# Wider token chunks in a two-FFN kernel, with a table of shifts for the order of its instructions

## The chip, the cores and the metric

The kernel runs on one core of one Trainium2 chip. The metric is the device time of one execution in microseconds (us), as a median of several runs. The engines are named as the profile names them: PE (TensorE, matmuls; PEld its weight loads), DVE (VectorE), ACT (ScalarE), POOL (GpSimd) and SP (SyncE, which here only starts DMAs). All of them run at the same time, each with a queue of instructions in a fixed order.

## The reference

Attention is followed by two feed-forward networks (FFNs) on the same 2304 tokens (4 batches of 576).

```python
scores = where(block_i >= block_j, q @ k.T / 8, -1e9)   # 4 x 8 heads, 576 tokens, 64 wide, blocks of 64
x = softmax(scores) @ v                                 # -> [2304, 512]
h = x @ w_in                                            # first FFN, 512 -> 1024
solu = h * softmax(h)
ln = (solu - mean) / sqrt(var + 1e-6) * g_ln
x = ln @ w_out                                          # 1024 -> 512
h = x @ w_in2                                           # second FFN, 512 -> 2048
out = (h * sigmoid(1.702 * h)) @ w_out2                 # 2048 -> 512
```

The inputs are handed over as 64-bit floats for the weights, so each weight matrix has to be put together from two 32-bit words on the chip. Both FFNs are computed with each operand as a sum of a high and a low part (H and L), three matmuls for one product: H by H, H by L and L by H.

## The kernel before

**How it is scheduled.** The program isn't issued as it is written. A class `Recorder` takes every operation with a priority (`_add`, L294; the priority is a time in us at which the work is due), and `issue` (L418) replays them through a model: `_cost` (L222) estimates each instruction, `HOP` the time of a semaphore between engines, `_room` (L114) gives out the 8 banks of PSUM, and of all operations the one with the earliest modelled start goes next, by priority where they tie. The result is a fixed order on each engine. Operations that can run on several engines (`copy`, `both`, `affine`) go to the one that the model sees done first. While the model is below `WARM` = 100 us, `_keep_busy` (L398) puts in idle 128-column matmuls, which read the tile `mask` and compute nothing, wherever the model sees PE without work for over 0.4 us. Because everything goes through `Recorder`, nearly every instruction stands under one line, L387, in the profile; tiles tell them apart.

**Attention** (`attention`, L986). 16 pairs of heads, four for each batch. `load_qk` (L709) and `load_v` load a pair; for the first batch first the tokens up to 256, then the rest, one pair after the other on SP's queue, and pair 0's k alone on ACT's. `scores` computes the products, `u_pt` transposes the softmax, `u_pv` multiplies with v. Raw q and k stand in four buffers (`rawb`, L602; the last one lies in the tile `x_all` of the first FFN).

**First FFN** (`first_ffn`, L1057). 18 tiles of 128 tokens. `h_mm` multiplies one tile with `w_in` (24 matmuls of 512 columns), `solu_ln` does the activation and the norm, `ln_t` (L955) transposes the tile into `lnTb`, and `y_mm` (L972) multiplies a chunk of `CH` = 256 tokens (two tiles) with `w_out`: for each of 9 chunks four calls of 24 matmuls, 256 columns each. Its result goes through the tiles `yo` to DRAM (`y1d`). Weights are converted by `w1_prep` through the landing tiles `e` and the tiles `wtmp` (L576).

**Second FFN.** Tokens go in four chunks, `sizes = [640, 512, 512, 640]` (L1135), and the 2048 hidden columns in 8 pairs of 256. A chunk of n tokens and one pair is computed by a scheme with 7 products instead of 8 (`h2_steps`, L1270): each product is 6 matmuls over half a chunk, n/2 columns, into one bank of PSUM, and DVE or ACT then reads it out (tiles `p`, `u`, `hc`); the activation goes through `sg` to the tiles `g` (H and L). `out_steps` (L1319) multiplies `g` with `w_out2`: for each 128 tokens of the chunk 6 matmuls of 512 columns, which accumulate over four pairs in one bank that is held for so long. The products of pair p+1 and the output steps of pair p are recorded interleaved. The pairs 0 to 3 go over all chunks in order first, then the pairs 4 to 7 over the chunks in reverse order. Where the chunk changes, `y_split` (L1253) writes the seven operands of the next one into their only set of tiles. `prep_w2` (L1215) makes the weights of a pair, `ahead` (L1197) converts those of later pairs and parks them in DRAM (`w2d`). There are three sets of `g` tiles (L1174, L1378), two or three `hc` and two `p`.

Of the kernel before, what the change touches and what calls it, by code (L numbers as in the profile page):

```python
# [2 lines left out]

# [18 lines left out]
def full(t):  # L22
    return t.bitcast(F32)

# [35 lines left out]
class Recorder:  # L60
# [5 lines left out]
    HOP = 0.06  # L66
    SPAN = 10
    OWN = 0.15
    LEAVE = (0, 1, 1)
    WARM = 100.0  # L70
    IDLE = 0.4
    SWITCH = 0.09
# [5 lines left out]
    def __init__(self, tc, banks):  # L78
# [4 lines left out]
        self.n_buf = 0  # L83
        self.places = {}
# [24 lines left out]
    def bank(self, level, n=1, name="b"):  # L109
        self.n_buf += 1  # L110
        b = Buf(n, level, f"{name} {self.n_buf}")
        return Bank(b, self.banks, (lambda t: t[:, 0]) if n == 1 else (lambda t: t[:, 0:n]))
# [109 lines left out]
    def _cost(self, eng, name, kw, outs, ins):  # L222


        out = kw.get("out")
        n = out.free_size() if callable(out.free_size) else out.free_size
        sb = [a for a in ins if a.space != PSUM]
        if eng == "tensor":
            if name == "transpose":
                return 0.109, 0.2, False  # L230
            k = kw["lhsT"].shape[0]
            if kw["lhsT"].dtype == F32:

                return max(0.109, 0.87 * n / 1000), 0.3 + (0.87 * n / 1000 if k == 64 else 0.0), False
            if k == 64:
                return max(0.054, 0.235 * n / 1000), 0.17 + 0.427 * n / 1000, False
            return max(0.109, 0.008 + 0.435 * n / 1000), 0.17 + 0.0 * n, False
        if name == "dma_start":
            return 0.48, 1.9, False
        if eng == "scalar":  # L240
            m = max((a.free_size() if callable(a.free_size) else a.free_size) for a in ins)
            c = 0.18 + 0.81 * m / 1000
            if kw["in_"].space != PSUM:
                c += 0.04
            if hasattr(kw.get("bias"), "partition_size"):
                c += 0.08
            if kw.get("accum_out") is not None:
                c += 0.19
            return c - 0.09, 0.09, False
        m = max([n] + [(a.free_size() if callable(a.free_size) else a.free_size) for a in ins])  # L250
        if eng == "vector":
            if name == "memset":
                return 0.06 + m / 1000, 0.05, False
            two = [a for k, a in kw.items() if k in ("in0", "in1", "in_") and a.space != PSUM
                   and (a.free_size() if callable(a.free_size) else a.free_size) > 1]
            port = len(two) == 2 or (len(two) == 1 and name in ("tensor_copy", "tensor_scalar"))
            c = 0.10 + 1.04 * m / 1000
            if kw.get("accum_out") is not None:
                c += 0.08
            return c, 0.07, port  # L260
        if name == "memset":
            return 0.07 + m / 1000, 0.05, False
        if name == "tensor_tensor":
            if kw["op"] == ALU.pow:
                return 0.55, 0.05, True
            return 0.2 + 2.4 * m / 1000, 0.05, True
        return 0.1 + 1.2 * m / 1000, 0.05, True
# [26 lines left out]
    def _add(self, forms):  # L294
# [7 lines left out]
        op.prio = self.prio  # L302
# [50 lines left out]
    def _wake(self, i):  # L353
        op = self.ops[i]
        op.ready = {}
        for e in op.forms:
            t = 0.0
            for eng, done, lag, _ in op.after:
                if eng == e:
                    t = max(t, done - lag if e == "tensor" else done)  # L360
                else:
                    t = max(t, done + self.HOP)
# [35 lines left out]
    def _keep_busy(self, mode, start):  # L398

        t = max(self.free["tensor"], 0.6)  # L400
        if self.idle is None or t > self.WARM:
# [100 lines left out]
def kernel(  # L502
# [29 lines left out]
    CH = 256  # L532
    TPC = CH // 128
    NC = NT // CH
# [12 lines left out]
    y1d = [dram.tile([DM, CH], F32, name=f"y1d{c}") for c in range(NC)]  # L547

    begun = const.tile([128, 1], F32, name="begun")
    tc.nc.scalar.activation(out=begun, in_=mhalf, func=ACTF.Exp)  # L550
# [6 lines left out]
    w1i_all = keep.tile([128, 2 * KD, FF1], F32R, name="w1i")  # L557
# [4 lines left out]
    x_all = keep.tile([128, 2560], F32, name="x")  # L562
    xs_all = keep.tile([128, 2048], F32R, name="xs")
    xb = [x_all[:, i * 512:i * 512 + 512].rearrange("p (k n) -> p k n", k=KD) for i in range(2)]
    rb = [mp.tile([128, KD, 128], F32, name=f"r{i}") for i in range(2)]
# [4 lines left out]
    eb = [mp.tile([128, 2, 512], F32, name=f"e{i}") for i in range(3)]  # L570
# [3 lines left out]
    yo_all = mp.tile([128, 3 * CH], F32, name="yo")  # L574
    yob = [yo_all[:, i * CH:(i + 1) * CH] for i in range(3)]
    wtmp = [yo_all[:, 0:512].bitcast(I32), junk.rearrange("p a b -> p (a b)").bitcast(I32)]  # L576
# [20 lines left out]

    NPTY = 1
# [3 lines left out]
    rawb = [ap1.tile([128, 2, S], F32, name=f"rawqk{i}") for i in range(3)]  # L602
    rawb.append(x_all[:, 1024:1024 + 2 * S].rearrange("p (n s) -> p n s", n=2))
# [12 lines left out]
    ptx = ap1.tile([128, 2, 384], F32, name="ptx")  # L616
# [14 lines left out]
    def ptx_of(p):  # L631

        return ptyb[0][:, :, 384 * (p - 1):384 * p] if early(p) else ptx
# [9 lines left out]
    def clear():  # L643
        nc.vector.memset(mask, 0.0)
        nc.idle = mask
        nc.vector.memset(mask[0:64, 448:512], -1e30)
        for t in vb:
# [78 lines left out]
    def split_qk(p):  # L726
# [4 lines left out]
        r = rawb[vat(p)]  # L731
# [72 lines left out]
    def scores(p, what):  # L804
# [4 lines left out]
        if p < NFULL:  # L809
            terms = [(rawb[vat(p)][:, 0], rawb[vat(p)][:, 1])]  # L810
# [144 lines left out]
    def ln_t(t, half):  # L955
# [3 lines left out]
        i = t % TPC  # L959
# [12 lines left out]
    def y_mm(cc, m):  # L972
        y = nc.bank(0, name="y")[:, 0:CH]
        H, L = lnTb
# [493 lines left out]
```

## Time and profile before

| what | us |
|---|---|
| median of 3 runs (lowest to highest) | 773.4 (772.5 to 773.99) |
| the profiled execution | 772.48 |
| its span, first to last instruction | 770.7 |
| PE busy | 763.0 |
| DVE, ACT, POOL busy | 526.6, 438.2, 288.2 |
| granted TensorE clock, share of full | 0.999 |

The profiled execution is one run; 1.8 us of it lie outside the span of the instructions. A matmul's busy time in the profile is longer than the distance to the next one, because matmuls overlap; the distance between starts is what they cost. Three stages can be told apart by the tiles: attention with the first FFN until about 260 us, the first FFN alone until about 377 us (its last `y_mm` run between the first products of the second FFN until 392 us), then the second FFN.

### The profile page before, as it was taken

The page shows a single profiled execution, that of the slowest core. Times are in us where ns is not written, and L with a number is a line of the kernel's source. Part 1 is how long each engine was busy: PE and PEld are TensorE (multiplying, and loading weights), DVE is VectorE, ACT ScalarE, POOL GpSimd, SP SyncE. Part 2 cuts the span into 40 slices and gives each one's busy share as a digit, 9 for nine tenths or more (in the row PEclk, how much of TensorE's full clock was granted, in tenths as well). Part 3 has the DMA queues.
Part 4 walks back from the last instruction along what each step waited for, and adds up shares of the span by engine and source line. Part 5 has one row for each costly group of instructions (what it writes and reads, how often), then busy time and mean ns, then how long its engine had stood idle before and what let it go on. Part 6 is the DMA issues. An engine that isn't in the chain of part 4 may idle for free.

```text
span 770.7 us, 14020 instructions
## 1 busy us (share of the span) xinstructions
PE 763.0 (99%) x4994; PEld 655.3 (85%) x4994; DVE 526.6 (68%) x1203; ACT 438.2 (57%) x1001; POOL 288.2 (37%) x359
## 2 busy tenths in 40 slices
PE   9999999999999999999999999999999999999998
PEld 6576777887878889989999899988899989999886
DVE  4989848557566578698458877668977564667544
ACT  6978957767675657567345645454555442435321
POOL 3525501223331264354122445464443221535311
PEclk9999999999999999999999999999999999999999
DMA  8876523531211346554502364456423030130201
GB/s 257 260 235 185 187 89 121 158 113 54 80 57 53 112 121 168 177 163 147 171 21 74 94 202 147 141 158 218 133 82 95 14 110 14 56 110 1 96 1 68
DMA packets 81431, 91.43 MB, mean 119 GB/s; under 512 B 11089, under 2 KB 58321, under 8 KB 81361
## 3 DMA queue, kind: packets, MB, share of 16 engines
q1 hardware_dynamic: 81216, 90.41, 38.0%
q8 instruction: 39, 0.64, 0.4%
q14 instruction: 32, 0.25, 0.1%
q10 hardware_dynamic: 144, 0.13, 0.1%
HBM read 66.59 MB, written 23.93 MB: 117 GB/s over the span
## 4 chain that ended last, share of the span: by engine, by line
PE 94%; ACT 1%; DMA 1%; DVE 1%; POOL 1%; issue 1%; SPq 0%; ACTq 0%; DVEq 0%
PE PS L387 94%; DMA land<-in_moe_w_out_dram 1%; ACT P L387 1%; DMA e<-in_moe_w_out_dram 0%; DVE w1o L387 0%; POOL xs L387 0%; POOL yo L387 0%; POOL e L387 0%; ACT e L387 0%; ACT pty L387 0%; POOL sg L387 0%; DVE e L387 0%; DVE ob L387 0%; DVE wt L387 0%; ACT wt L387 0%
## 5 line engine op out<-in xcount | busy, mean ns | idle before, releaser
L387 ACT ACTIVATE sg<-hc 128x320 f32<-128x320 f32 (+1 forms) x128 | 56.5, 442 | 108.4 <-DVE hc L387 94.3
L387 PE MATMUL PS<-w2oL,gH 128*128 128x512 f32 x288 | 113.1, 393 | 0.0
L387 PE MATMUL PS<-w2oH,gH 128*128 128x512 f32 x288 | 113.0, 392 | 0.0
L387 PE MATMUL PS<-w2oH,gL 128*128 128x512 f32 x288 | 112.1, 389 | 0.0
L387 PE MATMUL PS<-lnTH,w1o 128*128 128x256 f32 x576 | 109.3, 284 | 0.0
L387 PE MATMUL PS<-w1i,xs 128*128 128x512 f32 x432 | 108.4, 399 | 0.0
L387 PE MATMUL PS<-w1i,w2SH 128*128 128x320 f32 (+1 forms) x512 | 105.1, 295 | 0.0
L387 POOL TENSOR_TENSOR sg<-hc,sg 128x256 f32<-128x256 f32 (+1 forms) x54 | 46.1, 854 | 128.8 <-ACT sg L387 128.7
L387 PEld LDWEIGHTS PS<-w1i,xs 128*128 128x128 f32 x432 | 78.2, 188 | 17.2 <-issue 2.1
L387 PEld LDWEIGHTS PS<-lnTH,w1o 128*128 128x128 f32 x576 | 90.6, 188 | 1.6 <-issue 0.7
L387 PEld LDWEIGHTS PS<-w1i,w2SH 128*128 128x128 f32 x512 | 85.1, 190 | 3.8
L387 PE MATMUL PS<-lnTL,w1o 128*128 128x256 f32 x288 | 81.2, 282 | 0.0
L387 DVE TENSOR_TENSOR hc<-PS,u 128x320 f32<-128x320 f32 (+1 forms) x96 | 43.7, 456 | 52.9 <-PE PS L387 48.2
L387 DVE CUSTOM_DVE_ANT_0 P<-PS,mask 128x512 f32<-128x512 f32 (+3 forms) x128 | 57.1, 485 | 30.9 <-PE PS L387 30.6
L387 PE MATMUL PS<-w1i,w2SL 128*128 128x320 f32 (+1 forms) x256 | 75.8, 296 | 0.0
L387 ACT ACTIVATE P<-P,mx 128x256 f32<-128x256 f32 (+3 forms) x128 | 70.3, 551 | 9.0 <-DVE mx L387 8.9
L387 ACT ACTIVATE gH<-sg 128x320 fp32r<-128x320 f32 (+1 forms) x114 | 49.8, 442 | 32.3 <-DVE sg L387 24.8
L387 PEld LDWEIGHTS PS<-w2oH,gL 128*128 128x128 f32 x288 | 54.1, 188 | 12.5 <-DVE gL L387 0.6
L387 PEld LDWEIGHTS PS<-w2oH,gH 128*128 128x128 f32 x288 | 54.2, 188 | 9.0
L387 PEld LDWEIGHTS PS<-w2oL,gH 128*128 128x128 f32 x288 | 54.2, 188 | 8.1
L387 POOL TENSOR_TENSOR gL<-sg,gH 128x256 fp32r<-128x256 f32 (+1 forms) x44 | 36.6, 838 | 52.1 <-ACT gH L387 51.3
L387 DVE TENSOR_TENSOR gL<-sg,gH 128x320 fp32r<-128x320 f32 (+1 forms) x84 | 47.8, 574 | 11.5 <-ACT gH L387 9.8
(193 smaller groups left out, 1660.1 us busy)
## 6 DMA issues: line engine op xcount, KB each, us to landing
land<-in_moe_w_in_dram SPq DMA_DIRECT2D x16, 512.0 KB, 3.9
land<-in_moe_w_out_dram SPq DMA_DIRECT2D x16, 512.0 KB, 4.4
w2d<-wt SPq DMA_DIRECT2D x24, 256.0 KB, 2.2
wt<-w2d SPq DMA_DIRECT2D x24, 256.0 KB, 2.9
x<-y1d SPq DMA_DIRECT2D x10, 512.0 KB, 6.1
y1d<-yo SPq DMA_DIRECT2D x36, 128.0 KB, 1.9
e<-in_moe_w_in_dram SPq DMA_DIRECT2D x8, 512.0 KB, 4.2
r<-rcd SPq DMA_DIRECT2D x32, 128.0 KB, 3.8
```

The costliest lines, as they stand in the source:

```text
L387: getattr(getattr(self.nc, e), name)(*map(real, args), **{k: real(v) for k, v in kw.items()})
```

## The change

- `sizes` becomes three chunks of 768 tokens. A product then has 384 columns, and the output steps hold 6 banks of PSUM, which leaves two: `_room` gets a rule that at most two products are alive at a time, in the order in which they are recorded, in place of leaving one bank free.
- `TILES = [2, 2, 2, 3, 3, 3, 3]`: `y_mm` works on chunks of 256 or 384 tokens, 7 instead of 9. There are two `yo` tiles instead of three.
- The first loads: for the four pairs of the first batch q goes on SP's and k on ACT's queue, all q and k come ahead of all v, and the first activation (with the load of its table) is recorded behind them.
- To make room, tiles share memory: raw q and k have two tiles of their own and two in `x_all`, pairs from 4 on alternate between two; one of the `wtmp` lies in the x tile of the first FFN; `ptx` and the `r` tiles lie in `x_all`; the small tiles of the second FFN lie in the `e` tiles; there are two sets of `g` and one `p`. One output weight of pair 1 is parked in DRAM.
- The model's costs are changed (`_cost`, a `HOPS` for each engine, `SWITCH`), idle matmuls may be put in at any time (they read `ident` after the attention), and each recorded operation's priority is shifted by its entry of `SHIFT`, a table of 3084 numbers in hundredths of a us (5% to 95%: -23.9 to +22.5; mean size 13.3).

```diff
+SHIFT = np.frombuffer(zlib.decompress(base64.b85decode(
...
+)), "<i4") / 100
...
+    HOPS = {'tensor': 0.06, 'vector': 0.034, 'scalar': 0.034, 'gpsimd': 0.078, 'sync': 0.06}
-    WARM = 100.0
...
-        if len(free) - sum(b.n for b in bufs) < self.LEAVE[max(b.level for b in bufs)]:
+        if bufs[0].name.startswith("P "):
+            live = [b for b in self.products if b.at is None or b.left]
+            at = next(i for i, b in enumerate(live) if b.at is None)
+            if sum(b.at is not None for b in live) >= 2:
+                return None
+            if bufs[0] is not live[at] and any(b.at is not None for b in live[at:]):
+                return None
+        elif len(free) - sum(b.n for b in bufs) < self.LEAVE[max(b.level for b in bufs)]:
...
-        op.prio = self.prio
+        op.prio = self.prio + float(SHIFT[len(self.ops)])
...
-    CH = 256
-    TPC = CH // 128
-    NC = NT // CH
+    TILES = [2, 2, 2, 3, 3, 3, 3]
+    CH = 128 * max(TILES)
+    NC = len(TILES)
...
-    wtmp = [yo_all[:, 0:512].bitcast(I32), junk.rearrange("p a b -> p (a b)").bitcast(I32)]
+    wtmp = [xb[0].rearrange("p k n -> p (k n)").bitcast(I32), junk.rearrange("p a b -> p (a b)").bitcast(I32)]
...
-    rawb = [ap1.tile([128, 2, S], F32, name=f"rawqk{i}") for i in range(3)]
-    rawb.append(x_all[:, 1024:1024 + 2 * S].rearrange("p (n s) -> p n s", n=2))
+    rawb = [ap1.tile([128, 2, S], F32, name=f"rawqk{i}") for i in range(2)]
+    rawb += [x_all[:, 1280 + i * 2 * S:1280 + (i + 1) * 2 * S].rearrange("p (n s) -> p n s", n=2) for i in range(2)]
...
-            (nc.scalar if n and p == 0 and s.start == 0 else nc.sync).dma_start(out=rawb[vat(p)][:, n, s], in_=x[b, i, :, s])
+            (nc.scalar if n and p < NPB and s.start == 0 else nc.sync).dma_start(out=raw_qk(p)[:, n, s], in_=x[b, i, :, s])
...
         for p in range(NPB):
-            yield from load(p, first, vx)
-            if p == 0:
-                yield 0.0, (clear,)
+            yield 0.0, (load_qk, p, first)
+        yield 0.0, (clear,)
+        for p in range(NPB):
+            yield 0.0, (load_v, p, vx)
...
-    sizes = [640, 512, 512, 640]
+    sizes = [768] * 3
...
-    gb += [[[fp.tile([128, CM], F32R, name=f"g{x}{e}{i}") for x in "HL"] for e in range(2)] for i in (1, 2)]
...
+    gb += [[[fp.tile([128, CM], F32R, name=f"g{x}{e}{i}") for x in "HL"] for e in range(2)] for i in (1,)]
```

## Rows read from the trace of the kernel before

**Rows 1.** The page, busy time: us (share of the span) x instructions.
```profile
PE 763.0 (99%) x4994; PEld 655.3 (85%) x4994; DVE 526.6 (68%) x1203; ACT 438.2 (57%) x1001; POOL 288.2 (37%) x359
```
**Rows 2.** Busy time by stretch: length, then PE, PEld, DVE, ACT, POOL, clock, DMA, GB/s.
```profile
100.00:260.00 160.00, 159.74 (x1239) 127.01 (x1239) 96.88 (x298) 108.59 (x285) 41.94 (x60) 1.00 0.30 88
375.00:520.00 145.00, 145.00 (x914) 133.14 (x913) 101.28 (x196) 73.58 (x162) 61.28 (x74) 1.00 0.38 121
520.00:545.00 25.00, 24.41 (x142) 22.10 (x141) 22.66 (x34) 11.93 (x26) 14.58 (x14) 1.00 0.63 213
545.00:767.00 222.00, 221.91 (x1275) 199.38 (x1273) 139.19 (x295) 92.68 (x203) 72.23 (x81) 1.00 0.19 61
```
**Rows 3.** Instructions by form on PE: count, busy us, mean ns, idle before.
```profile
L387 PE MATMUL PS<-lnTH,w1o 128*128 128x256 f32 x576 | 109.3, 284 | 0.0
...
L387 PE MATMUL PS<-w1i,w2SH 128*128 128x320 f32 x256 | 57.1, 308 | 0.0
...
L387 PE MATMUL PS<-mask 128*128 128x128 f32 x58 | 10.2, 322 | 2.0 <-DVE mask L387 1.5 <-DVE mx L387 0.6
```
**Rows 4.** Timeline of PE, 256 columns in `y_mm`: start, us, instruction (12 steps apart).
```profile
298.12 0.29 PE L387 MATMUL PS<-lnTL,w1o 128*128 128x256 f32 x1
...
299.56 0.29 PE L387 MATMUL PS<-lnTL,w1o 128*128 128x256 f32 x1
```
**Rows 5.** Timeline of PE, products of 320 columns (6 steps apart).
```profile
561.84 0.31 PE L387 MATMUL PS<-w1i,w2SL 128*128 128x320 f32 x1
...
562.72 0.31 PE L387 MATMUL PS<-w1i,w2SL 128*128 128x320 f32 x1
```
**Rows 6.** Timeline of PE, output steps of 512 columns (12 steps apart).
```profile
450.05 0.39 PE L387 MATMUL PS<-w2oH,gL 128*128 128x512 f32 x1
...
452.77 0.39 PE L387 MATMUL PS<-w2oH,gL 128*128 128x512 f32 x1
```
**Rows 7.** Timeline of the start: loads (SPq, ACTq), idle matmuls, first uses.
```profile
0.72 0.40 ACTq L387 DMA_DIRECT2D rawqk<-in_k_dram  x1
...
1.47 2.93 PE L387 MATMUL PS<-mask 128*128 128x128 f32 x12 [1.47 <-DVE mask L387]
...
2.14 0.43 SPq L387 DMA_DIRECT2D rawqk<-in_k_dram  x1
...
5.07 0.44 SPq L387 DMA_DIRECT2D x<-in_k_dram  x1
...
5.69 0.40 ACT L387 ACTIVATE P<-P,mx 128x128 f32<-128x128 f32 x1 [3.04 <-DVE mx L387]
...
6.34 0.93 PE L387 MATMUL PS<-rawqk 64*128 64x128 f32 x8
...
10.21 0.93 PE L387 MATMUL PS<-x 64*128 64x128 f32 x8
```
**Rows 8.** Busy time by stretch in the first 85 us, columns as in rows 2.
```profile
8.00:12.00 4.00, 4.00 (x37) 2.73 (x36) 2.53 (x19) 2.13 (x10) 0.27 (x1) 1.00 0.92 287
12.00:16.00 4.00, 4.00 (x27) 2.27 (x27) 2.22 (x8) 3.70 (x17) 2.38 (x5) 1.00 1.05 342
...
60.00:85.00 25.00, 23.57 (x172) 14.31 (x171) 23.66 (x68) 22.14 (x53) 15.13 (x20) 1.00 0.73 209
```
**Rows 9.** The chain that ended last, around the weights' conversion: start, us, what.
```profile
64.04 3.73 DMA e<-in_moe_w_out_dram
...
79.16 0.61 DVE pty L387
```
**Rows 10.** Timeline at a change of chunk: POOL, DVE and PE.
```profile
523.51 1.99 POOL L387 TENSOR_TENSOR w1i<-x,w1i 128x640 fp32r<-128x640 f32 x1
...
524.01 1.78 DVE L387 TENSOR_TENSOR gL<-sg,gH 128x256 fp32r<-128x256 f32 x1
...
536.03 0.42 PE L387 MATMUL PS<-xs,w2BH 128*128 128x320 f32 x1 [0.58 <-POOL xs L387]
```
**Rows 11.** Instructions by form on DVE, 560 to 622 us: a product's read-out.
```profile
L387 DVE TENSOR_TENSOR hc<-PS,u 128x320 f32<-128x320 f32 x14 | 6.9, 491 | 13.1 <-PE PS L387 12.8
```

More of the change, by code (lines that the diff above doesn't have):

```diff
@@ L83, in __init__ @@
         self.n_buf = 0
+        self.products = []
         self.places = {}
@@ L111, in bank @@
         b = Buf(n, level, f"{name} {self.n_buf}")
+        if name == "P":
+            self.products = [x for x in self.products if x.at is None or x.left] + [b]
         return Bank(b, self.banks, (lambda t: t[:, 0]) if n == 1 else (lambda t: t[:, 0:n]))
@@ L238, in _cost @@
         if name == "dma_start":
             return 0.48, 1.9, False
+        m = max([n] + [size(a) for a in ins])
+        accum = kw.get("accum_out") is not None
         if eng == "scalar":
[L241 to L248, printed above, removed]
@@ L261, in _cost @@
-        if name == "memset":
-            return 0.07 + m / 1000, 0.05, False
+            m = max(size(a) for a in ins)
+            c = 0.054 + 0.82 * m / 1000 if kw["in_"].space == PSUM else 0.092 + 0.836 * m / 1000
+            if accum:
+                c += 0.188
+            scaled = hasattr(kw.get("scale"), "partition_size")
+            if scaled:
+                c += 0.09
+                if hasattr(kw.get("bias"), "partition_size") and not accum:
+                    c += 0.09
+            return c, 0.115, False
@@ L531 @@
     scale = 1.0 / float(D) ** 0.5
-    CH = 256
-    TPC = CH // 128
-    NC = NT // CH
+    TILES = [2, 2, 2, 3, 3, 3, 3]
+    CH = 128 * max(TILES)
+    NC = len(TILES)
+    ENDS = [sum(TILES[:c + 1]) for c in range(NC)]
+    Y1 = [(128 * (e - n), 128 * n) for e, n in zip(ENDS, TILES)]
     NTILE = NT // 128
@@ L546 @@
     rcd = [dram.tile([2 * NPB, S], F32, name=f"rcd{b}") for b in range(B)]
-    y1d = [dram.tile([DM, CH], F32, name=f"y1d{c}") for c in range(NC)]
+    y1d = [dram.tile([DM, n], F32, name=f"y1d{c}") for c, (_, n) in enumerate(Y1)]
     begun = const.tile([128, 1], F32, name="begun")
-    tc.nc.scalar.activation(out=begun, in_=mhalf, func=ACTF.Exp)
     nc = Recorder(tc, psum.tile([128, 8, 512], F32, name="PS"))
@@ L561 @@
     mp = m_es.enter_context(tc.tile_pool(name="mp", bufs=1, side="left"))
[L562 to L563 removed]
+    x_all = keep.tile([128, 3584], F32, name="x")
+    xs_all = wx_all[:, 2 * KD * FF1:]
     xb = [x_all[:, i * 512:i * 512 + 512].rearrange("p (k n) -> p k n", k=KD) for i in range(2)]
[L565 removed]
+    rb = [x_all[:, 1024 + i * 512:1536 + i * 512].rearrange("p (k n) -> p k n", k=KD) for i in range(2)]
     xHL = [[
@@ L569 @@
     ] for j in range(2)]
-    eb = [mp.tile([128, 2, 512], F32, name=f"e{i}") for i in range(3)]
+    e_all = keep.tile([128, 3 * 1024], F32, name="e")
+    eb = [e_all[:, i * 1024:(i + 1) * 1024].rearrange("p (a b) -> p a b", a=2) for i in range(3)]
     stb = [mp.tile([128, 8], F32, name=f"st{i}") for i in range(3)]
@@ L1148 @@
     part = [dram.tile([n, DM], F32, name=f"part{i}") for i, n in enumerate(sizes)]
-    w2d = {i: dram.tile([4, 128, 512], F32, name=f"w2d{i}") for i in range(2, NPAIR)}
+    w2d = {i: dram.tile([4, 128, 512], F32, name=f"w2d{i}") for i in range(1, NPAIR)}
     land = [m2_p.tile([128, 1024], I32, name=f"land{i}") for i in range(2)]
@@ L1195, in convert, with ahead @@
         return t.bitcast(F32)
-    def ahead(pair):
-        for j in range(4):
+    def ahead(pair, todo=range(4)):
+        for j in todo:
             t = convert(pair, j)
@@ L1203, in raw @@
     def raw(pair, j):
-        if pair not in w2d:
+        if pair == 0 or pair == 1 and j < 2 + EARLY:
             return convert(pair, j)
@@ L1215, in prep_w2, with prep_in @@
     def prep_w2(pair):
-        A, Bw, Sw, O = slots[pair % NSLOT]
+        prep_in(pair)
+        for e in range(2):
+            prep_out(pair, e)
+    def prep_in(pair):
+        A, Bw, Sw = slots[pair % NSLOT]
         F0, F1 = (raw(pair, j) for j in range(2))
@@ L1227, in prep_w2, with prep_out @@
             hl([x[:, 2 * e:2 * e + 2] for x in Sw], stmp[:, 2 * e:2 * e + 2])
-        for e in range(2):
-            hl(O[e], raw(pair, 2 + e)[:, 0])
+    def prep_out(pair, e):
+        hl(slots_out[pair % NSLOT][e], raw(pair, 2 + e)[:, 0])
     def y_load(cc):
@@ L1357 @@
     nc.floor = max(op.done for op in nc.ops if op.tag == "A")
-    for p in range(2):
-        nc.prio = f_time + P0 + PI * p
-        prep_w2(p)
+    nc.prio = f_time + P0
+    prep_w2(0)
+    nc.prio = f_time + P0 + PI
+    prep_in(1)
+    for e in range(EARLY):
+        prep_out(1, e)
+    ahead(1, range(2 + EARLY, 4))
     for p in range(2, NSLOT):
```

230 lines of the change are left out of this document (166 added, 64 removed).

## Prediction

> **What bounds the kernel now.** I read the page's busy times first: PE is busy for 763.0 of 770.7 us, every other engine for 68% or less [rows 1]. Busy alone proves little for overlapping matmuls, so the second view is the busy time by stretch: from 100 us on PE has no gap that matters but in one stretch, 520 to 545 us, where 0.6 us are missing while DVE is busy for 22.7 of 25 us [rows 2]. The third is the timeline, for the distance between starts of matmuls. It is regular: 12 steps of 256 columns take 299.56 - 298.12 = 1.44 us, 0.1200 us each [rows 4]; 6 steps of 320 columns 0.88 us, 0.1467 each [rows 5]; 12 steps of 512 columns 2.72 us, 0.2267 each [rows 6]. All three lie on one line: columns / 2400 us + 0.0133 us. So from 100 us on the time is the sum of PE's matmuls, and each has a fixed part of 13.3 ns beside its columns. The first 85 us are another stage: 58 idle matmuls on `mask` stand there, 10.2 us busy [rows 3], the stretch 60 to 85 us lacks 1.4 us of PE with DVE at 23.7 and ACT at 22.1 of 25 us [rows 8], and at 64 us the chain leaves PE for a load of `w_out`, its conversion and DVE, and comes back only after 79 us [rows 9]. There PE waits for the other engines.
>
> **Fewer, wider matmuls.** The columns stay as they are; what goes is the fixed part. Second FFN: a chunk needs 8 pairs x 7 products x 6 = 336 matmuls, so 4 chunks have 1344 and 3 have 1008. (The count can be checked on one form: 2 chunks of 640 x 8 pairs x 4 products with `w2S` x 4 matmuls with its H half = 256 [rows 3].) 336 x 13.3 ns = **4.5 us less**. First FFN: `y_mm` has 9 x 96 = 864 (the 576 of rows 3 are the two of three with `lnT`'s H half), now 7 x 96 = 672: 192 x 13.3 ns = **2.6 us less**. The trace shows no 384 columns, but sizes on both sides of it; I take the line's 0.1733 us. Both stages are PE's own, so all 7.1 us should show.
>
> The Trainium skill, "TensorE: Matmul & The Clock Gate", section "Wait — 56ns, not 53.3ns?", speaks against so much: it gives back-to-back matmuls a fixed part of about 2.5 ns. By it, as an estimate, this term would be 528 x 2.5 ns = 1.3 us in place of 7.1. The trace doesn't agree, with 13.3 ns at three sizes [rows 4 to 6], and the measurement decides.
>
> **Two banks for the products.** Six banks are held, so a product may start only when the last but one has been read out. A pair now takes 42 x 0.1733 + 36 x 0.2267 = 15.4 us with 7 products in it, one every 2.2 us. Product i+2 starts 4.4 us after product i, which itself takes 1.04 us: 3.4 us are left for the read-out. That takes 491 ns for 320 columns [rows 11], so about 0.6 us for 384; it fits nearly six times, if DVE comes at once. It doesn't at a change of chunk: POOL's 640-column subtraction takes 1.99 us, DVE's 256-column operation beside it 1.78 us, over three times its 320-column one of rows 11, and later PE waits 0.58 us for `xs` [rows 10]. At 768 columns POOL's would be about 2.4 us. One such block fits into 3.4 us, two in a row don't: 2 x 2.4 + 0.6 - 3.4 = 2.0 us lost. Before there were 6 changes of chunk and one lost time; now there are 4, but the beginning of the second FFN has such work too. Bounds: 0.6 us gained if the loss of rows 2 goes, 5 x 2.0 = 10 us lost if two blocks meet at each of the 5 places. I take **1 us more**, near the row of before, since output steps can fill in.
>
> Two sets of `g` instead of three: the output steps of pair p-1 run beside the products of pair p, and the first write for pair p+1 comes three products later, so two sets do while both stay level; a lag is priced in the 10 us above. `p` is free again after two more products, which follow within the pair. DVE, ACT and POOL get fewer and longer instructions over the same elements, and DVE stands at 139 of 222 us in the last stretch [rows 2], so none becomes the bound. Pair 1's parked weight adds two transfers of 256 KB on SP's queue, at a DMA share of 0.38 [rows 2]; the two `yo` tiles are filled only every 24 x 0.1733 = 4.2 us; the last pair's chain and its stores stay as they are: nothing for these three.
>
> **The first loads.** Pair 1's k is issued at 2.14 us and used at 6.34; pair 3's at 5.07 and 10.21 [rows 7]: 4.2 and 5.1 us from issue to use. With k on ACT's queue at 0.4 us each, all eight are issued by 0.72 + 4 x 0.4 = 2.3 us, so pair 3 could start at about 7, 3 us earlier. But the exponentials begin at 5.69 [rows 7], and what the start gains ends where ACT is full: it is idle for 4 - 2.13 = 1.9 us from 8 to 12 us and for 0.3 from 12 to 16 [rows 8]. Bounds: nothing, and 3 us. I take ACT's idle time, **2.0 us less**. What is moved: ACT issues four transfers instead of one, so the load of its table starts some 1.2 us later and should be over near 4 us, before the first exponential at 5.69; only those are queued behind it. The v loads, and those of weights behind them, come after all four q on SP's queue; pair 0's v would be issued at about 2.5 and, at 5 us from issue to use, be there by 8; its products come after the transposes, and pair 3's scores at 10.21 were still ahead of them before.
>
> The DMA engines move 287 GB/s from 8 to 12 and 342 from 12 to 16 us [rows 8], so they are full whoever issues. The Trainium skill, "DMA: Bandwidth & Descriptors", section "Issuing engines are not separate DMA queues", says that transfers started by several engines run on the same DMA engines, and only the time to start them is saved. By it, as an estimate, this term would be three starts of 0.4 us, 1.2 us instead of 2.0.
>
> **The order.** New costs and shifts of some 10 us reorder all that is within reach of a product or two, on every engine. What an order can win is PE's waste in front: 10.2 us of idle matmuls without the 2.9 before the first data [rows 3, 7], and the 1.4 us missing from 60 to 85 us [rows 8]; less the 2.0 just taken, 6.7 us. It can lose as well, and the trace of before has no row for the new order: shared tiles tie the conversions of weights (`wtmp` in the x tile) to the loading of tokens. Bounds: 6.7 us gained, and 8 lost, one more conversion in the chain (half of 64 to 79 us [rows 9]). The amount of conversion stays. I take **1.8 us less**, a quarter of the gain, since the engines at their limit from 60 to 85 us keep all their work.
>
> **Sum.** 772.5 - 4.5 - 2.6 + 1.0 - 2.0 - 1.8 = 762.6 us for the profiled execution. The median of the runs stands 0.9 us above it (773.4), so the forecast is **763.5 us**.
>
> **Rivals.**
> - The front empties: the order wins all 6.7 us and the changes of chunk give back 0.6 instead of costing 1: 763.5 - 4.9 - 1.6 = 757.0 us. For it: PE's only losses are there. Against: DVE at 95% from 60 to 85 us [rows 8]. Chance 0.17, from 755 to 760.
> - The two banks bite: half of their bound, 5 us instead of 1, 767.5 us. For it: rows 10. Against: the output steps that can fill. Chance 0.14, from 767 to 771.8.
> - Slower: the shared tiles put conversions in series. Place: 30 to 85 us, `wtmp`, `ptx` and raw q and k in the x tile. Each more in the chain costs 8 us [rows 9]: one gives 771.5, two 779.5, and it is slower than before from the second on. For it: the chain runs through them for 15 us. Against: half of the conversions use another tile. Chance 0.05.
> - It doesn't save what it says: the fixed part grows with the columns, so that 384 cost as much as the narrower ones did for each column, and all 7.1 us stay: 770.6 us. Against: three sizes on one line. Chance 0.02. (By the page on TensorE, as an estimate, it would be 769.3.)
>
> The forecast itself, 760 to 767, has 0.62.
>
> **How the numbers follow.** The range 757.5 to 769.5 leaves out half of the first rival, a third of the second, all of the third and the fourth: 0.085 + 0.045 + 0.05 + 0.02 = 0.2. A measurement of this kernel can tell about 0.2%, 1.5 us, from no change. Faster than 771.9: 0.62 + 0.17 + 0.14 + 0.02 = 0.95, of which I put 0.03, the upper edge of the second and fourth, within: 0.92. Within 0.03, slower than 774.9 0.05.
>
> **What would show it.** 1008 product matmuls 0.173 us apart, 672 of `y_mm`; pairs 15.4 us apart in the second FFN; the fourth pair's scores near 7 to 8 us; fewer idle matmuls before 85 us; PE's gaps in the second FFN below 2 us. It would be wrong if steps of 384 columns are longer, if DVE reads products out over 3.4 us late at a change of chunk, or if the conversions of `w_out` end later than before.

## The result, and the profile after

| | before | after |
|---|---|---|
| median of four runs each, us | 772.95 (772.2 to 773.99) | 761.47 (761.34 to 761.86) |
| profiled execution, its span, us | 772.48, 770.7 | 761.34, 759.6 |
| PE matmuls | 4994 | 4444 |
| idle matmuls on `mask` | 58 | 36 |

The changed kernel is faster: 0.9845 of the time before, with an interval of 0.983 to 0.986. That is 1.5%, 11.5 us between the medians and 11.1 us between the two profiled spans; this section takes the 11.1 us apart. The forecast was 763.5 us. The granted clock is 0.999 in the profile before and 1.0 in the one after, the upper of the two levels (2.4 GHz), so the clock explains nothing here. In the experiments below all executions are counted, except that one execution of `e10_table_back`, of 1930 us where the other nine lie between 772.8 and 775.8, is left out of its ratio.

The page of after, busy time of each engine, its share of the span, and instructions (answers [rows 1]):

```profile
PE 752.3 (99%) x4444; PEld 648.1 (85%) x4444; DVE 507.7 (67%) x1072; ACT 422.8 (56%) x926; POOL 288.9 (38%) x328
```

PE is still the bound, with 550 matmuls fewer: 528 as counted in the prediction and 22 idle ones. DVE has 131 instructions fewer and is busy 18.9 us less, 67% of a shorter span. PE's instructions by form in after (form, count, busy us, mean ns, idle time ahead of them; answers [rows 3]):

```profile
L488 PE MATMUL PS<-w1i,w2SH 128*128 128x384 f32 x384 | 98.0, 336 | 0.0
L488 PE MATMUL PS<-lnTH,w1o 128*128 128x384 f32 x256 | 67.9, 341 | 0.0
L488 PE MATMUL PS<-lnTL,w1o 128*128 128x384 f32 x128 | 43.4, 339 | 1.2 <-DVE lnTL L488 1.2
L488 PE MATMUL PS<-lnTH,w1o 128*128 128x256 f32 x192 | 39.4, 291 | 0.0
L488 PE MATMUL PS<-lnTL,w1o 128*128 128x256 f32 x96 | 27.0, 281 | 0.0
L488 PE MATMUL PS<-mask 128*128 128x128 f32 x36 | 6.5, 351 | 1.5 <-DVE mask L488 1.5
```

The four forms of `y_mm` add up to 672, as counted. The products, of which one form of 384 is shown, add up to 1008. Busy time by stretch in after (columns as in [rows 2]):

```profile
60.00:85.00 25.00, 24.95 (x179) 16.48 (x179) 23.05 (x71) 23.41 (x58) 15.51 (x20) 1.00 0.55 173
100.00:260.00 160.00, 160.00 (x1233) 130.59 (x1232) 92.49 (x281) 113.12 (x294) 46.25 (x62) 1.00 0.35 100
360.00:400.00 40.00, 38.84 (x218) 37.36 (x217) 19.63 (x27) 14.02 (x27) 10.96 (x10) 1.00 0.32 112
400.00:740.00 340.00, 339.36 (x1696) 305.55 (x1695) 229.56 (x383) 149.61 (x280) 115.27 (x112) 1.00 0.29 94
```

Against [rows 8], 60 to 85 us lacks 0.05 us of PE instead of 1.4 and holds 179 matmuls instead of 172, while the DMA share fell from 0.73 to 0.55. A gap stands now at 360 to 400 us, where 1.16 us are missing. The timeline of after, at the start, at six steps of products and at that gap (start, length, engine, operation, count, idle time and its releaser):

```profile
1.16 0.97 ACTq L488 DMA_DIRECT2D rawqk<-in_k_dram  x2
1.47 5.71 PE L488 MATMUL PS<-mask 128*128 128x128 f32 x32 [1.47 <-DVE mask L488]
7.11 0.93 PE L488 MATMUL PS<-rawqk 64*128 64x128 f32 x8
9.06 0.40 ACT L488 ACTIVATE P<-P,mx 128x128 f32<-128x128 f32 x1 [4.92 <-DVE mx L488]
...
362.57 0.33 PE L488 MATMUL PS<-w1i,w2AL 128*128 128x384 f32 x1
362.74 0.51 PE L488 MATMUL PS<-w1i,w2AH 128*128 128x384 f32 x2
363.09 0.34 PE L488 MATMUL PS<-w1i,w2AL 128*128 128x384 f32 x1
...
363.62 0.42 PE L488 MATMUL PS<-lnTH,w1o 128*128 128x384 f32 x1
365.20 0.44 PE L488 MATMUL PS<-lnTL,w1o 128*128 128x384 f32 x1 [1.16 <-DVE lnTL L488]
...
562.14 0.51 PE L488 MATMUL PS<-w1i,w2BH 128*128 128x384 f32 x2
...
563.19 0.51 PE L488 MATMUL PS<-w1i,w2SH 128*128 128x384 f32 x2
```

Three things are to be seen. The scores begin at 7.11 us, behind one block of 32 idle matmuls, and the first exponential at 9.06, where before had it at 5.69 [rows 7]. Three steps of 384 columns take 363.09 - 362.57 = 0.52 us, 0.173 each, which is the line's value; over all steps of 384 columns in the trace the median is 0.174 us. And after the first `lnTH` step at 363.62 the next one starts only at 365.20: it waits for DVE's `lnTL`.

**The 11.1 us by stage.** To split them I gave each matmul its columns at 2400 per us plus 13.3 ns (the small forms, transposes and scores, their own regular step; an idle matmul on `mask` nothing, but one on `ident`, which only the experiments have, its step of 0.109 us) and added them up: 730.7 us before, 723.7 after. The difference is 7.0 us, 528 x 13.3 ns. What the span has beyond that sum is lost time, 40.0 us before and 35.9 after. Since I assign the 13.3 ns, the 7.0 us are a sum from the steps just read and not a measurement of their own, and the split by stage moves by some tenths of a us with the steps taken for the small forms. By stage, from the start times of PE's instructions:

| stage, us | lost before | lost after | change |
|---|---|---|---|
| 0 to 20 | 9.2 | 8.5 | -0.7 |
| 20 to 65 | 4.3 | 2.2 | -2.1 |
| 65 to 85 | 5.4 | 1.4 | -4.0 |
| 85 to 260 | 13.7 | 11.7 | -2.0 |
| 260 to 400 | 0.7 | 3.2 | +2.5 |
| 400 to 740 | 2.6 | 5.0 | +2.4 |
| 740 to the end | 4.1 | 3.9 | -0.2 |

So by this sum fewer matmuls give 7.0 us, the front up to 260 us 8.8, and 260 to 740 us takes 4.9 back.

### The profile page after: what moved, and what is told of

Its sections match the earlier page's. It is cut to its first block, busy times and chain, and to the rows that moved or that the text cites. A ratio compares the mean times of both kernels' runs of the same rounds, so it can differ in the third digit from the quotient of the medians.

```text
span 759.6 us, 12556 instructions
## 1 busy us (share of the span) xinstructions
PE 752.3 (99%) x4444; PEld 648.1 (85%) x4444; DVE 507.7 (67%) x1072; ACT 422.8 (56%) x926; POOL 288.9 (38%) x328
## 4 chain that ended last, share of the span: by engine, by line
PE 95%; DVE 3%; ACT 1%; issue 0%; POOL 0%; ACTq 0%; DVEq 0%; POOLq 0%
PE PS L488 95%; DVE lnTL L488 0%; DVE e L488 0%; ACT e L488 0%; DVE yL L488 0%; DVE wt L488 0%; ACT P L488 0%; DVE gL L488 0%; DVE sg L488 0%; ACT junk L488 0%; POOL st L488 0%; DVE w2BL L488 0%; DVE w1i L488 0%; ACT PR L488 0%; DVE land L488 0%
## 5 line engine op out<-in xcount | busy, mean ns | idle before, releaser
L488 DVE TENSOR_TENSOR e<-PS,e 128x384 f32<-128x384 f32 x168 | 90.7, 554 | 92.8 <-PE PS L488 89.4
L488 PE MATMUL PS<-w1i 128*128 128x512 f32 (+1 forms) x456 | 113.5, 394 | 0.0
L488 PE MATMUL PS<-lnTH,w1o 128*128 128x384 f32 (+1 forms) x448 | 107.3, 319 | 0.0
L488 PE MATMUL PS<-w1i,w2SH 128*128 128x384 f32 x384 | 98.0, 336 | 0.0
L488 PEld LDWEIGHTS PS<-w1i 128*128 128x128 f32 x456 | 83.0, 188 | 16.5 <-issue 1.2
L488 ACT ACTIVATE P<-P,mx 128x128 f32<-128x128 f32 (+3 forms) x128 | 71.0, 558 | 7.5 <-DVE mx L488 7.5
L488 DVE CUSTOM_DVE_ANT_0 P<-PS,mask 128x128 f32<-128x128 f32 (+3 forms) x128 | 57.4, 485 | 24.6 <-PE PS L488 24.1
L488 PE MATMUL PS<-lnTL,w1o 128*128 128x384 f32 (+1 forms) x224 | 70.5, 315 | 1.2 <-DVE lnTL L488 1.2
L488 PE MATMUL PS<-w1i,w2SL 128*128 128x384 f32 x192 | 64.5, 336 | 0.3 <-DVE w2SL L488 0.3
L488 PE MATMUL PS<-ident,P 128*128 128x128 f32 x320 | 45.8, 277 | 0.2 <-ACT P L488 0.2
```

The costliest lines, as they stand in the source:

```text
L488: getattr(getattr(self.nc, e), name)(*map(real, args), **{k: real(v) for k, v in kw.items()})
```

## Experiments

The theory after the result was: the fixed part of the matmuls is worth 7 us, the order (the table of shifts) empties the front, and the wide chunks cost something in the second FFN. The rivals: the new costs of the model or the two queues do what I give to the table; and the fixed part isn't what the widths save. Ratios are against the kernel before, run on the same chip beside each, whose medians were 772.66 us (`e1` to `e4`), 773.07 (`e5` to `e8`) and 773.6 (`e9` to `e12`). So a difference of medians between these groups carries up to 1 us from the chips.

### The table off, sizes and tiles put back one by one

`e1_no_table` has only this edit:

```diff
-        op.prio = self.prio + float(SHIFT[len(self.ops)])
+        op.prio = self.prio + 0.0
```

> The changed kernel with all entries of the table of shifts at zero; chunks, costs, loads and memory as changed. If the table made the better order of the first 85 us (6.8 us less lost there than before), most of that comes back: 766 to 769 us, and the conversions of w_out stand in the chain again around 64 to 80 us. If the new costs or the moved buffers made it, the time stays within 1 us of 761.5.

Measured: 775.85 us (774.57 to 778.52), ratio 1.0046 (1.003 to 1.0061). Without the table the change is slower than the kernel before; the table is worth 14.4 us by the medians, 15.5 by the ratios. Where they go is in the stretches (columns as before) and in PE's waits (us in total, times, longest) of `e1_no_table`:

```profile
60.00:85.00 25.00, 22.62 (x167) 13.65 (x163) 22.66 (x72) 21.60 (x59) 16.15 (x20) 1.00 0.73 213
400.00:740.00 340.00, 335.81 (x1675) 301.31 (x1675) 224.81 (x358) 152.44 (x285) 146.82 (x127) 1.00 0.30 94
```

```profile
PE PS L488 <- DVE e L488: 3.8, 3, 2.0
```

60 to 85 us lacks 2.4 us of PE (before 1.4), and 400 to 740 us lacks 4.2, with the read-out of products by DVE (`e`) as the releaser. The longest of these waits, in the timeline of `e1_no_table`:

```profile
572.20 1.36 DVE L488 TENSOR_TENSOR gL<-e,gH 128x384 fp32r<-128x384 f32 x1
...
573.49 1.75 DVE L488 TENSOR_TENSOR w2SL<-stmp,w2SH 128x512 fp32r<-128x512 f32 x1
...
575.16 1.01 DVE L488 TENSOR_TENSOR e<-PS,e 128x384 f32<-128x384 f32 x2
...
575.76 0.62 PE L488 MATMUL PS<-w1i,w2SH 128*128 128x384 f32 x2 [1.98 <-DVE e L488]
```

Two long DVE operations in a row stand ahead of the read-out, and PE has no free bank for the next product. By the same sum as above it loses 17.5 us up to 85 us (before 18.9, after 12.1) and 9.0 from 400 to 740 (before 2.6, after 5.0).

`e2_no_table_old_sizes` is `e1_no_table` with the old chunks of the second FFN:

```diff
-    sizes = [768] * 3
+    sizes = [640, 512, 512, 640]
```

> As e1_no_table, and the second FFN again in chunks of 640, 512, 512 and 640 tokens (the rule of two products alive stays). If each matmul has a fixed 13.3 ns, 336 more make 4.5 us more than e1_no_table, give or take what the order changes in stalls; the sum of starts-to-starts in the second FFN shows it without them. If the wider chunk gained by something else (fewer changes of chunk, fewer reads), the steps of 320 and 256 columns don't stand on the line with 384.

Measured: 774.69 us, ratio 1.0021 (1.0012 to 1.0031), 1.2 us under `e1_no_table`. From 400 to 740 us it loses 3.4 us instead of 9.0, with the rule for two products still in place. By that sum the 768-token chunks save their 4.5 us of fixed part and lose more than that when the order isn't made for them.

`e3_no_table_old_tiles` is `e1_no_table` with the old tiles of the first FFN:

```diff
-    TILES = [2, 2, 2, 3, 3, 3, 3]
+    TILES = [2] * 9
```

> As e1_no_table, and the first FFN's second product in 9 chunks of 256 tokens. The fixed part alone: 192 matmuls more, 2.6 us more than e1_no_table. If chunks of three tiles cost stalls at the end of the first FFN (1.4 us in the changed kernel), the difference is only about 1.2 us, or none.

Measured: 778.39 us, ratio 1.0066 (1.0045 to 1.0088): 2.5 us over `e1_no_table`. That fits the 2.6 us of the wider tiles, but the two intervals overlap, so it isn't clear of noise.

`e4_no_table_old_both` has both edits.

> As e1_no_table, with the old chunks in both places: what is left of the change are costs, loads and memory. By the fixed part 7.1 us more than e1_no_table. If costs, loads and memory bring nothing without the table, this is the kernel before, 772.5 to 774 us.

Measured: 780.53 us, ratio 1.0102 (1.0087 to 1.0117). The four kernels make a square. By the medians, tiles bring 5.8 us with the old sizes and 2.5 with the new; sizes bring 2.1 with the old tiles and cost 1.2 with the new; both together bring 4.7, not 7.1. Only the 5.8 and the 4.7 are well clear of noise, and each corner has an order of its own from the planner. The rest of the change (shared memory, first loads, the rule for two products, idle matmuls at any time) stands in this last kernel alone and costs 7.9 us against the kernel before. Its trace has 42 idle matmuls on `ident` that before doesn't have, at their step of 0.109 us 4.6 us in all; the other three corners have 8, 12 and 2, so up to 3.7 us of the 4.7 may be idle matmuls and not widths. No run took them out.

### The new costs alone

`e7_before_new_costs` is the kernel before with the new `_cost`, `HOPS` and `SWITCH`, and nothing else:

```diff
+    HOPS = {'tensor': 0.06, 'vector': 0.034, 'scalar': 0.034, 'gpsimd': 0.078, 'sync': 0.06}
...
-    SWITCH = 0.09
+    SWITCH = 0.1
...
-            return max(0.109, 0.008 + 0.435 * n / 1000), 0.17 + 0.0 * n, False
+            return max(0.0675, 0.008 + 0.435 * n / 1000), 0.163, False
```

> The kernel before with the model's new costs and hops alone. If the new costs made the better order of the first 85 us, 766 to 768 us with less lost there; if the table did, 772 to 775.

Measured: 772.61 us, ratio 0.9996 (0.9987 to 1.0006): the same as before. Better costs of the model bring nothing by themselves. Whether they have a part in the 7.9 us above, together with the rest, wasn't tested.

### One half of the table at a time

`e9_table_front` uses the shifts only for what is recorded up to the end of the first FFN (the attention with it), `e10_table_back` only for the second FFN:

```diff
-        op.prio = self.prio + float(SHIFT[len(self.ops)])
+        op.prio = self.prio + (float(SHIFT[len(self.ops)]) if self.front else 0.0)
...
+    nc.front = False
```

> The changed kernel with the table's entries for the operations of attention and first FFN alone (the first 1684); those of the second FFN are zero. The order until about 260 us is that of the changed kernel. If the table's 14.4 us lie in front, 762 to 764 us; if they lie in keeping the second FFN with its two banks free of stalls, 768 to 775 us, with losses after 360 us as in e1_no_table.

> The other half: zero for attention and first FFN, the table's entries for the second FFN alone. If the entries only fit the whole order for which they were made, this is no better than e1_no_table and may be far worse (stalls of tens of us in the second FFN); if the second FFN's order is worth the half of the 14.4 us on its own, 768 to 770 us.

Measured: 772.34 us, ratio 0.998 (0.9968 to 0.9993), and 774.47 us, ratio 1.0017 (1.0005 to 1.0028). Of the table's 14.4 us the front half alone brings 3.5 and the back half alone 1.4 by the medians; by the ratios, which leave the chips' difference out, 5.1 and 2.2 of 15.5. The lost time shows why the parts don't add up:

| lost, us | before | after | no table | front half | back half |
|---|---|---|---|---|---|
| up to 260 us | 32.6 | 23.8 | 32.6 | 23.6 | 33.5 |
| 400 to 740 us | 2.6 | 5.0 | 9.0 | 6.3 | 5.1 |
| idle matmuls on `ident` | 0 | 0 | 8 | 74 | 36 |

Each half does its own stage: the front half empties the front as far as the whole table does, the back half takes the second FFN to where after has it. (The idle matmuls on `ident` count as work here; of the front half's 74, 22 lie behind 400 us, 2.4 us on top of the 6.3.) Busy time from 60 to 85 us and one of PE's forms in `e9_table_front`:

```profile
60.00:85.00 25.00, 24.96 (x180) 16.46 (x180) 23.09 (x72) 23.40 (x58) 15.79 (x20) 1.00 0.55 178
```

```profile
L489 PE MATMUL PS<-ident 128*128 128x128 f32 x74 | 9.3, 276 | 0.5 <-DVE e L489 0.5
```

Around the seam between the halves (301 to 411 us) the planner finds PE without ready work in its model and puts idle matmuls in: 74 x 0.109 = 8.1 us, most of the 10.1 us by which its span (769.7 us) is longer than that of after; in `e10_table_back` they stand at 310 to 314 us. That they are a cost of the seam, and not of either half, is only read from the two traces; no run took them out alone.

### The width of a product by itself

`e5_split` keeps the order of every engine and issues each product's matmul as two of 192 columns, so 1008 matmuls more over the same columns:

```diff
+                halves = [slice(0, 192), slice(192, 384)]
+        for s in halves:
...
+                    args, kw = (args[0][:, s],), kw | dict(rhs=kw["rhs"][:, s])
```

> The changed kernel with each product of the second FFN in two accumulation groups of 192 columns, the same order otherwise: 1008 matmuls more over the same columns. If the fixed part is 13.3 ns at any width, 192 columns step by 0.0933 us and the kernel takes 13.4 us more: 775. By a fixed part of 2.5 ns it would be 2.5 us more: 764. If a weight load sets a floor above 0.093 us, more than 13.4.

Measured: 808.2 us, ratio 1.0457 (1.0438 to 1.0476), 46.7 us over after: 46 ns for each added matmul, not 13.3. The timeline of `e5_split`, steps of 192 columns:

```profile
559.79 0.27 PE L497 MATMUL PS<-w1i,w2SH 128*128 128x192 f32 x1
559.90 0.27 PE L497 MATMUL PS<-w1i,w2SL 128*128 128x192 f32 x1
...
561.24 0.27 PE L497 MATMUL PS<-w1i,w2BL 128*128 128x192 f32 x1
561.35 0.41 PE L497 MATMUL PS<-w2oH,gH 128*128 128x512 f32 x1
```

From 559.79 to 561.24 are 13 steps, 0.1115 us each; the line through 256, 320 and 512 columns would give 0.0933. Six steps of 384 in after take 563.19 - 562.14 = 1.05 us, 0.175 each. Two halves cost 2 x 0.1115 - 0.175 = 0.048 us more than the whole, and 1008 x 0.048 = 48 us, which is the measured difference within 2 us. So PE sets the pace there step by step, as the prediction took it, but the line can't be carried below 256 columns. For the change itself that is of no matter, since it goes from 256 and 320 to 384 columns, all on the line.

### One queue, and the start

`e6_one_queue` records the k loads of pairs 1 to 3 on SP's queue, with the table kept:

```diff
-            (nc.scalar if n and p < NPB and s.start == 0 else nc.sync).dma_start(out=raw_qk(p)[:, n, s], in_=x[b, i, :, s])
+            (nc.scalar if n and p == 0 and s.start == 0 else nc.sync).dma_start(out=raw_qk(p)[:, n, s], in_=x[b, i, :, s])
```

> The changed kernel with k of pairs 1 to 3 on SP's queue again, the order of the program as it is. If two queues bring the start its time, up to 1.5 us more than 761.5. If the DMA engines are the bound in the first 10 us whoever issues, no difference beyond 0.5 us.

Measured: 851.85 us, ratio 1.1038 (1.1 to 1.1076). That isn't the price of a queue. Stretches and PE's waits in `e6_one_queue`, and its chain that ended last (start, us, what):

```profile
440.00:515.00 75.00, 19.43 (x59) 15.65 (x58) 31.33 (x52) 16.09 (x27) 10.59 (x15) 0.53 0.46 140
520.00:560.00 40.00, 38.77 (x196) 34.56 (x195) 23.63 (x37) 19.57 (x37) 22.11 (x16) 1.00 0.24 80
```

```profile
PE PS L488 <- ACT e L488: 45.9, 3, 45.1
```

```profile
459.79 0.32 SPq L488
460.20 3.92 DMA land<-in_moe_w_in_dram
464.23 0.67 ACT wt L488
464.89 0.07 issue
464.96 0.65 POOL land L488
465.64 0.71 DVE land L488
466.43 0.70 DVE wt L488
```

Three loads that were moved at 2 us make PE stand still for 55 us around 440 to 515 us. The chain is there a series of weight conversions of the second FFN, each of a load, ACT, POOL and DVE. By that chain, the order computed from this program with the other program's shifts puts those conversions ahead of the work that PE waits for. The question about the queues stays unanswered by this run.

`e8_wide_first` turns the tiles round, to see whether the three-tile wait at 363.62 us goes when the wide chunks come first:

```diff
-    TILES = [2, 2, 2, 3, 3, 3, 3]
+    TILES = [3, 3, 3, 3, 2, 2, 2]
```

> The changed kernel with the chunks of the first FFN's second product as 3, 3, 3, 3, 2, 2, 2 tiles. The matmuls are as many. If PE's wait of 1.4 us near 364 us is due to three tiles being transposed at once at the end, it falls to about half and the time is 0.5 to 1 us less, unless the table, made for the other order, costs as much elsewhere.

Measured: 953.4 us, ratio 1.2335 (1.2316 to 1.2354), again with a table made for another program. PE's waits in `e8_wide_first`:

```profile
PE PS L488 <- DVE e L488: 101.5, 34, 72.5
```

The wait for `lnTL` is shorter there (0.4 us), but with 101.5 us of other waits around it that proves nothing. This one is inconclusive.

The next two therefore keep every engine's order as after has it: the instructions are collected in the order issued, edited, and then issued. `e11_order_kept_one_queue` moves the start of three k loads to SP, at the same places:

```diff
+        ks = [i for i, (e, c) in enumerate(kept) if e == "scalar" and c[0][0] == "dma_start"]
+        for i in ks[1:] if not self.edits else ():
+            kept[i] = "sync", kept[i][1]
```

> The changed kernel with every engine's order kept as it is, and the three k loads of pairs 1 to 3 started by SP at the same places of the order. If starting loads on two queues is worth what is saved in starts, 3 x 0.43 us, the first scores come about 1 us later than 7.1 and the time is 762 to 763 us. If the DMA engines are the bound, less than 0.4 us.

Measured: 762.44 us (762.0 to 762.81), ratio 0.986 (0.9843 to 0.9876): 1.0 us over after. The timeline of `e11_order_kept_one_queue`:

```profile
2.62 0.43 SPq L495 DMA_DIRECT2D rawqk<-in_k_dram  x1
4.51 0.43 SPq L495 DMA_DIRECT2D x<-in_k_dram  x1
7.73 0.93 PE L495 MATMUL PS<-rawqk 64*128 64x128 f32 x8
...
554.80 0.62 PE L495 MATMUL PS<-w1i,w2SH 128*128 128x384 f32 x2 [0.56 <-DVE e L495]
```

The scores begin 0.6 us later (7.73 against 7.11). PE's matmuls have the same order as in after, so the two traces can be laid side by side: the delay is 0.7 us at 100 us, 0.6 at 400, and rises to 1.5 us only at 554.80 us, where PE waits 0.56 us for DVE in the second FFN, far from any load of q or k. So what belongs to the queue is 0.6 to 0.7 us of the 1.4 us between the profiled spans (761.0 and 759.6). Three starts of 0.43 us are 1.3 us. The intervals of the two ratios overlap and the times nearly touch (761.86 and 762.0), so by the runs alone the size isn't clear of noise.

`e12_order_kept_pair1_first` loads pair 1's q and k first and drops 9 idle matmuls (18 of the trace's records) ahead of its scores:

```diff
+            for e, a, b in (("scalar", ("x", 3008), ("rawqk1", 576)), ("sync", ("x", 1280), ("rawqk1", 0))):
+                i, j = at(e, *a), at(e, *b)
+                kept[i], kept[j] = kept[j], kept[i]
...
+            del kept[first - 9:first]
```

> The changed kernel with every engine's order kept, but pair 1's q and k change places with the two loads that stand first (pair 2's q and pair 3's k), since pair 1's scores are first in PE's order; of the 16 idle matmuls ahead of them 7 stay. If the start at 7.1 us is the wait for pair 1's loads, the scores begin at about 4.6 us. If the front is bound by ACT and DVE from there on, the kernel gains 1 to 2.5 us: 759 to 760.5. If the weights' loads and conversions bound the front, the gain is lost again before 85 us: 761.5.

Measured: 761.64 us (760.77 to 763.14), ratio 0.9852 (0.9831 to 0.9872): the same as after. Its timeline:

```profile
4.58 0.93 PE L495 MATMUL PS<-rawqk 64*128 64x128 f32 x8
7.01 3.56 PE L495 MATMUL PS<-x 64*128 64x128 f32 x28 [1.51 <-DMA x<-in_q_dram]
8.28 0.40 ACT L495 ACTIVATE P<-P,mx 128x128 f32<-128x128 f32 x1 [4.14 <-DVE mx L495]
```

PE has scores 2.5 us earlier and then waits 1.51 us for the next pair's q; the first exponential comes 0.8 us earlier. Laid side by side with after, PE stays 0.7 to 0.9 us ahead from there to the end (span 758.9 against 759.6). The runs scatter over 2.4 us, so their median can't show a gain of that size.

## Why the prediction was right, point by point

- **PE bounds the kernel: right.** PE is at 99% in both. `e5_split` shows it directly for the second FFN: what is added to PE's steps appears whole in the time.
- **Fewer, wider matmuls, -7.1 us: right in size, incomplete in its condition.** The counts were met, and the step at 384 columns is 0.173 us, as read off the line; the rival by which 384 columns cost as much a column as narrower ones falls with that. The Trainium skill, "TensorE: Matmul & The Clock Gate", section "Wait — 56ns, not 53.3ns?", gives a fixed part of about 2.5 ns; by that page, as an estimate, the term would have been 1.3 us. The trace doesn't agree at 384 columns either, where the median step of 0.174 us is 14 ns over the columns' 0.160. The words "so all 7.1 us should show" were too strong: without the table, sizes and tiles together brought 4.7 us (`e1_no_table` against `e4_no_table_old_both`), and the 768-token chunks by themselves between 2.1 us gained and 1.2 lost. PE's own saving shows whole only where the order then keeps PE fed. No run has a table made for the old widths, so what the widths bring under a fitted order is the sum of steps, not a measured difference.
- **Two banks for the products, +1.0 us: mis-sized.** From 400 to 740 us the loss rose by 2.4 us. 1696 matmuls in 340 us make a pair (78) last 15.6 us against the 15.4 of the prediction. It isn't one block of two slow instructions, as I had priced it. Two stalls of 0.5 us near 420 and 727 us cost about as much as before's stalls at its change of chunk near 525 to 536 us, 1.1 to 1.2 us by the same sum; the rest is steps of products and output steps a ns or two longer than before's against the line (0.175 us at 562 us), over some 1700 of them. What adds those wasn't separated. The mechanism is there, though: with no table the same stretch loses 9.0 us, PE's largest releaser is then the read-out by DVE, and its longest wait, 1.98 us, stands behind two long DVE operations in a row, the block that I had priced at 2.0. The second rival's 5 us would have been a fair price for that kernel.
- **A wait that I hadn't named.** A chunk of three tiles needs half as much again of `lnT` before its first `y_mm`, and at 363.62 us PE waits for it. The chain that ended last in after shows what DVE did ahead of the wait at 363.62 us (start, us, what):

```profile
356.44 2.34 DVE wt L488
358.78 2.51 DVE yL L488
361.29 0.60 DVE lnTL L488
361.89 0.87 DVE w1i L488
362.76 2.40 DVE lnTL L488 x4
365.16 0.04 issue
```

  DVE does a weight conversion and the first operands of the second FFN, and only then most of the low halves that PE waits for: a step of 1.58 us instead of 0.17, so 1.4 us. It is over half of the 2.5 us by which the loss between 260 and 400 us rose. I had written of the wider tiles only what they save, and priced no wait for their transposes. But three tiles alone don't make it. `e1_no_table` has the same chunks of three tiles and no idle time of PE ahead of that form (form, count, busy us, mean ns, idle time):

```profile
L488 PE MATMUL PS<-lnTL,w1o 128*128 128x384 f32 x128 | 43.3, 339 | 0.0
```

  So the wait comes with the order that the table makes, in which DVE's other work stands first there. Which of its shifts do that isn't known, and `e8_wide_first` doesn't tell whether another order of the tiles would avoid it.
- **The first loads, -2.0 us: mis-sized.** Up to 20 us the loss fell by 0.7 us. The two queues are worth 0.6 to 0.7 us in the trace of `e11_order_kept_one_queue`. The step that failed was the sequel: I took the pairs' scores to begin as early as before, with only pair 3 sooner. In after they begin at 7.11 us, all in one block, since the loads that come first belong to different pairs. `e12_order_kept_pair1_first` has pair 1's scores 2.5 us earlier and keeps 0.7 us of it: the rest goes where PE waits for the next pair's q. So there the gain ended at a load, and that it "ends where ACT is full" isn't shown. The Trainium skill, "DMA: Bandwidth & Descriptors", section "Issuing engines are not separate DMA queues", says that only the time to start a transfer is saved; by it, as an estimate, the term was 1.2 us. The run shows 0.6 to 0.7 us, about half of that.
- **The order, -1.8 us: the largest mis-sized term.** From 20 to 260 us the loss fell by 8.1 us, more than the upper bound of 6.7 that I had for it. The chain through the load of `w_out` [rows 9] is gone: after has no idle matmul behind 14 us, where before had 8 at 25 us and 14 between 69 and 77, and 60 to 85 us lacks 0.05 us of PE. Taking a quarter of the gain "since the engines at their limit from 60 to 85 us keep all their work" was the error: DVE and ACT are about as busy there as before (23.05 and 23.41 of 25 us, against 23.66 and 22.14 [rows 8]), and PE is fed all the same, since the work that it waits for comes early enough. My bound was too low as well, as it counted idle matmuls and gaps in two places of the front; by the sum above 2.0 us more came from 85 to 260 us, where PE is busy almost throughout [rows 2] and which I had taken to hold nothing. Which shifts remove the chain isn't known; that they are those of the front is shown by `e9_table_front`, that the new costs don't do it by `e7_before_new_costs`.
- **The sum.** The terms beside the fixed part were -2.8 us and turned out as -4.1: 1.3 us more from all of them, with the order 6.3 us better than taken, the first loads 1.3 worse, the wide chunks and tiles 3.9 worse (by stage; the wait at 363.62 us comes from the order as well), and 0.2 at the end better. The forecast was close partly because these errors go against each other. The first rival came half true: the front emptied by all that it had (8.8 us, against 6.7 and 2.0), and the second FFN took back more, not less.
- **The slower rival** had the wrong place. I put it into shared tiles before 85 us. Without the table the kernel is slower than before, by 0.46%, and its front is no worse than before's: up to 260 us it loses the same 32.6 us, and the rest goes in the second FFN (9.0 us against 2.6 from 400 to 740 us). How near that lay to the forecast couldn't be read from the trace of before, and a chance of 0.05 rested on the table being fit, which I hadn't said.
- **Signs named ahead.** Counts, steps of 0.173 us, fewer idle matmuls and PE's gaps in the second FFN (0.6 of 340 us) were met. "Conversions of `w_out` end later" told nothing: the last load of that weight in the front starts at 89.96 us in after and 90.14 before, while `h_mm` starts 6.5 us later (50.3 against 43.8 us) and ends 22.1 us earlier (342.2 against 364.3). A later start of one stage says nothing when another one fills PE.

## What to carry to other kernels

Read the fixed part of a matmul from the distance of starts at several widths in the trace, count the matmuls that go, and take the product for an upper bound: it shows whole only if the order keeps PE fed with the banks and buffers that the wider chunk leaves. Ask which neighbour in time has to deliver more before a wider step can begin (here DVE, which writes the transposes of three tiles) and what the order puts ahead of it, as that wait isn't in the old trace. A table of shifts belongs to exactly one program, so test one edit of such a kernel with every engine's order held fixed; otherwise the test measures the misfit, here 90 to 190 us. With the order fixed, lay the two traces side by side matmul by matmul: a delay that appears far from the edit isn't the edit's.

## What the runs showed of the hardware that I had not expected

- Steps of matmuls don't fall along the line below 256 columns: 0.1115 us at 192 columns against 0.0933. The Trainium skill, "TensorE: Matmul & The Clock Gate", section "Back-to-back issue gap", says that the loading of weights and the matmul set the spacing together, and gives about 81 ns at 128 columns and 131 ns at 512. A spacing above the line at 192 columns would fit that, but what sets it wasn't separated; the figure for 512 doesn't agree, with 0.2267 us here [rows 6].
- In `e6_one_queue` the granted clock is 0.53 from 440 to 515 us, nearly the lower level (1.2 GHz, 0.5), while PE is busy 19.4 of 75 us, and 1.00 again from 520 us on. In before and after PE never stands still so long, and the clock stays at 1.0.
